# Attention groups merged across batches and put between W2-W1 pairs of waves, with z summed over j on VectorE and batch 0's first chunk ahead of all else

## The chip, the cores and the metric

The kernel runs on one core of a Trainium2 chip. The metric is the device time of one execution in microseconds (us). Most executions of a kernel agree closely, but some are longer (of eleven of the kernel before, run beside z_twice_b1, ten took 138.85 to 139.62 us and one 140.37). A run counts as *slow* when it is more than 1.5% above the fastest run of the same kernel, otherwise as *fast*. Ratios are made from fast runs alone; a median quoted for an experiment is that of all its runs. A kernel is called faster or slower when it differs by more than 2%.

A profile is one traced execution. The span inside it (first to last instruction) is about 2 us shorter than the timed value (136.9 of 139.2 us before).

## The reference

There are two parts, one after the other, all in float32 in and out.

```python
# attention without softmax: q, k, v are (B=4, H=4, S=1088, D=32); S1, S2 are (8, 32)
def phi(x):                                   # 8 x 8 = 64 features
    a = einsum('rd,bhsd->bhsr', S1, x)
    b = einsum('rd,bhsd->bhsr', S2, x)
    return einsum('bhsi,bhsj->bhsij', a, b).reshape(..., 64)
q_p, k_p = phi(q), phi(k)
kv  = einsum('bhsf,bhsd->bhfd', k_p, v)
z   = sum(k_p, axis=2)                        # over the sequence
num = einsum('bhsf,bhfd->bhsd', q_p, kv)
den = einsum('bhsf,bhf->bhs', q_p, z)[..., None] + 1e-06
x   = (num / den), heads side by side         # (4352 tokens, 128)

# feed-forward: w_in (128, 2048), w_out (2048, 128), beta (2048,)
h = x @ w_in
g = h / (1 + exp(-beta * h))
out = g @ w_out
```

## The kernel before

The kernel folds beta into the weights, so that ScalarE applies a plain silu. The second part is cut into 68 *waves*. A wave is one W1 step (two matmuls of 512 tokens by 128 hidden units into PSUM), one silu of 128x1024 on ScalarE (about 1.02 us each), and later one W2 step (two matmuls that add to the output). The kernel sets `manual_schedule` for TensorE, VectorE and ScalarE, so that their instruction order is the order of the program text. So the kernel interleaves by hand: the function `slot` issues a wave and one attention group.

An attention batch is made of these groups:

- `kps` projects k; VectorE turns the result (`kab`) and multiplies the two halves into the 64 features, `kp`. In `kp` the sequence lies as 9 pieces j on up to 128 partitions.
- `ab` makes the two projections of q: `aps`, which ScalarE copies to `asb`, and `bps`, which VectorE multiplies with it into `qp`. There are four pairs per batch: two chunks of the sequence by two pairs of heads.
- `kv` adds up kv and z in one PSUM tile `kvz`: for each j and head one matmul with v and one with a block of ones.
- `ndt` transposes kv and z, `den` makes the denominator (matmuls `dps`, then five VectorE steps in a row to its reciprocal `rb`), and `num` makes the numerator `nps` and the product `xT`. The waves of those tokens can start once `xT` is there.

```python
psm = tile_pool("psm", bufs=2, PSUM)     # "wave": W1 tiles and aps share two buffers
pso = tile_pool("pso", bufs=1, PSUM)     # "moeout": the output sums
ps2 = tile_pool("ps2", bufs=1, PSUM)     # "two": kps, bps, nps
ps1 = tile_pool("ps1", bufs=1, PSUM)     # "one": kvz, ndps, dps
...
def slot(group=None):                    # wave, then group, then W2 of earlier waves
    if moe["ci"] < len(tok_chk) and sum(tok_chk[moe["ci"]]) <= moe["ready"]:
        w1()
    if group is not None:
        group()
    todo = moe["todo"]
    if len(todo) == 2 and todo[0][1] == 0 and todo[0][0] > 0:
        return
    while len(todo) > 1:
        w2(*todo.pop(0))
...
# in kv: z by matmuls with ones
for j in j_list:
    kr = 64 if j == 0 else P
    for which in range(2):
        for h in range(H):
            nc.tensor.matmul(
                out=kvz[32 * h : 32 * h + 32, F * which : F * which + F],
                lhsT=v_t[b][:kr, h, j, :] if which == 0 else ones[:kr, :],
                rhs=kp[:kr, h, j, :], ...)
...
# the first chunk of batch 0
kps()
for h in range(H): outer(h, 0, 5)
ab((0, 0), None)()
for h in range(H): outer(h, 5, NJK)
ab((1, 0), (0, 0))()
prep_rbeta()
keep_warm(4)
kv([1, 2, 3, 4])()
ab(None, (1, 0))()
kv([5, 6, 7, 8, 0])()
...                                      # weights scaled on GpSimd
keep_warm(2); ndt(); turn_q(0, 1); keep_warm(2)
den(0)(); num(0)()
keep_warm(6)
...
for b in range(1, B):
    slot(kps)
    outer(0); outer(1)
    slot(ab((0, 0), None))
    outer(2)
    slot(ab((1, 0), (0, 0)))
    outer(3)
    turn_q(b, 1)
    slot(kv([1, 2]))
    slot(ab((0, 1), (1, 0)))
    slot(kv([3, 4]))
    slot(ab((1, 1), (0, 1)))
    slot(kv([5, 6]))
    slot(ab(None, (1, 1)))
    turn_k(b + 1)
    slot(kv([7, 8, 0]))
    slot(ndt)
    slot(den(0))
    slot(num(0))
    slot(den(1))
    slot(num(1))
    turn_q(b + 1, 0)
    slot()
while moe["ci"] < len(tok_chk):          # the drain: waves only
    slot()
```

`keep_warm(n)` issues n matmuls whose results nobody uses; they only keep TensorE busy.

## Time and profile before

| | before |
|---|---|
| timed, median (3 runs) | 139.22 us (139.01 to 139.24) |
| span in the profile | 136.9 us |
| first wave starts | 21.7 us |
| busy: TensorE / ScalarE / VectorE | 117.5 / 80.9 / 64.0 us |

The page's busy times of the kernel before (engine, busy us, share of the span, instructions; PEld is the load of the stationary operand, which overlaps PE: 117.5 and 46.5 us in a span of 136.9):

```profile
PE 117.5 (86%) x1407; PEld 46.5 (34%) x1407; DVE 64.0 (47%) x127; ACT 80.9 (59%) x96; POOL 11.6 (8%) x25
```

An average over the span hides the stages, so the span is cut where the `xT` of a batch's second chunk is done. Busy times by windows, before (from:to, its length, then the busy us of each engine with the number of instructions, the granted TensorE clock, the share of DMA engines busy, GB/s):

```profile
0.00:21.72 21.72, 17.72 (x242) 7.18 (x243) 12.12 (x33) 4.33 (x11) 8.03 (x19) 1.00 0.94 301
...
30.72:57.42 26.70, 22.86 (x327) 8.97 (x328) 15.48 (x30) 16.02 (x19) 0.00 (x0) 1.00 0.26 56
57.42:84.84 27.42, 25.57 (x340) 9.78 (x339) 15.47 (x30) 18.64 (x22) 0.00 (x0) 1.00 0.14 21
84.84:112.26 27.42, 25.57 (x340) 9.78 (x339) 14.25 (x28) 18.65 (x22) 0.00 (x0) 1.00 0.14 20
112.26:131.88 19.62, 17.00 (x85) 8.00 (x84) 1.44 (x3) 16.83 (x18) 0.00 (x0) 1.00 0.28 41
```

The lines are: the start, batches 1, 2 and 3, and the drain. In batch 2 TensorE (the first pair of numbers) is busy for 25.6 of 27.4 us and the others far less. In the drain each of 18 silu takes 1.09 us from start to start. ScalarE is busy for 1.02 us of that and waits 0.26 us for a wave after every second silu, so it all but sets the pace.

The chain of waits that ended last, before, in the start and around the denominators of batch 2 (start us, length us, what; "xN" instructions taken together):

```profile
11.86 0.67 DVE qp L368
12.53 0.17 DVE rbeta L184
...
12.75 1.64 PE kvz L386 x64
...
15.03 1.39 PE kvz L386 x80
...
21.72 0.61 PE wave L242 x2
...
77.31 0.69 PE dps L433 x8
...
79.05 0.79 DVE rb L449
...
79.94 0.77 DVE xT L475
...
80.75 0.59 PE wave L242 x2
```

The first `kvz` waits until 12.75 us for `rbeta`, the reciprocal of beta, which stands on VectorE behind a product `qp`. It needs the result of neither; `rbeta` holds it up because the transposed beta lies in the one PSUM buffer that `kvz` takes next. (Each float32 matmul of `kvz` stands in these views as two records: the program has 72 per batch, the trace 144.) From `dps` at 77.3 to the wave at 80.75 us the chain runs over VectorE, with TensorE having little to do. Only part of that shows up as a wait, since TensorE does have an `nps` and some wave work in between. The waits of TensorE, before (engine line <- what ended the wait: us in all, times, longest us):

```profile
PE wave L242 <- DVE xT L475: 3.9, 4, 2.1
PE moeout L206 <- ACT g L250: 2.7, 9, 0.7
PE wave L242 <- ACT g L250: 2.1, 4, 0.6
```

Of the 3.9 us, 0.5 are at the first wave, 2.1 in batch 1 and 0.6 in each of batches 2 and 3.

### The profile page before, as it was taken

Reading aid. Unit: us, or ns where it says so; the run is one execution under the profiler, and the core shown is the slowest. Engines: PE = TensorE matmul, PEld = TensorE weight load, DVE = VectorE, ACT = ScalarE, POOL = GpSimd, SP = SyncE. Lnnn points to the kernel's source line nnn. Section 1 sums busy time; section 2 is a strip of 40 time slices with the busy share of each in tenths; the row PEclk is TensorE's granted clock in tenths of the full one; section 3 lists DMA queues with packets and bytes.
Section 4 is the critical chain, followed back from the end, with each engine's and each line's share of the span. In section 5 each row is a group of like instructions: output and inputs, shape, how many; then the busy total and the mean of one; then the engine's idle time right before and its main releaser. Section 6 shows DMA issues by size and latency. Waiting matters only on the chain.

```text
span 136.9 us, 3341 instructions
## 1 busy us (share of the span) xinstructions
PE 117.5 (86%) x1407; PEld 46.5 (34%) x1407; DVE 64.0 (47%) x127; ACT 80.9 (59%) x96; POOL 11.6 (8%) x25
## 2 busy tenths in 40 slices
PE   5698986989889984998989989989899898889850
PEld 2124632323333431224334322233344233333530
DVE  0687273499642535976245459772423570100210
ACT  3411104766776632677675756776757478888940
POOL 4000599300000000000000000000000000000000
PEclk9999999999999999999999999999999999999999
DMA  4999999999441000140004001400130004022042
GB/s 141 293 293 416 379 325 262 260 222 254 77 66 25 0 5 0 17 62 5 0 10 71 1 0 20 62 0 5 19 58 5 0 13 63 0 43 41 10 66 38
DMA packets 22814, 12.41 MB, mean 91 GB/s; under 512 B 18688, under 2 KB 20752, under 8 KB 22544
## 3 DMA queue, kind: packets, MB, share of 16 engines
q1 hardware_dynamic: 22736, 12.19, 36.4%
q8 instruction: 11, 0.18, 0.6%
q14 instruction: 3, 0.02, 0.1%
q10 hardware_dynamic: 64, 0.01, 0.1%
HBM read 9.97 MB, written 2.23 MB: 89 GB/s over the span
## 4 chain that ended last, share of the span: by engine, by line
PE 59%; DVE 22%; ACT 10%; issue 3%; DMA 2%; ACTq 1%; DVEq 0%
PE moeout L206 18%; PE wave L242 17%; ACT g L250 10%; PE kvz L386 8%; PE aps L353 4%; DVE kp L327 3%; DVE rb L449 3%; PE dps L433 3%; PE bps L353 3%; PE kps L308 3%; DVE xT L475 3%; DVE qp L368 3%; DVE dT L442 2%; DMA sraw<-in_S_dram 2%; DVE o_sb L216 2%
## 5 line engine op out<-in xcount | busy, mean ns | idle before, releaser
L250 ACT ACTIVATE g<-wave 128x1024 f16<-128x1024 f32 x68 | 68.7, 1023 | 38.5 <-PE wave L242 38.1
L242 PE MATMUL wave<-xT,winp 128*128 128x512 f16 (+1 forms) x144 | 40.2, 367 | 6.0 <-DVE xT L475 3.9
L206 PE MATMUL moeout<-g,woutp 128*128 128x512 f16 (+1 forms) x144 | 39.8, 369 | 3.6 <-ACT g L250 2.7
L368 DVE TENSOR_TENSOR qp<-bps,asb 128x576 f32<-128x576 f32 (+1 forms) x16 | 11.6, 725 | 25.4 <-PE bps L353 24.4
L242 PEld LDWEIGHTS <-winp 128*128 128x128 f16 x144 | 13.7, 97 | 25.0 <-issue 12.4
L206 PEld LDWEIGHTS <-woutp 128*128 128x128 f16 x144 | 10.9, 97 | 23.7 <-issue 18.8
L216 DVE STREAM_TRANSPOSE o_sb<-moeout 128x512 f32<-128x512 f32 (+1 forms) x9 | 6.1, 673 | 22.1 <-PE moeout L206 22.1
L386 PE MATMUL kvz<-kp,v 128*32 128x64 f32 (+1 forms) x288 | 11.2, 232 | 1.4 <-DVE kp L327 1.1
L353 PE MATMUL aps<-qT,s_164 32*64 32x288 f32 (+1 forms) x128 | 12.2, 448 | 0.0
L363 ACT COPY asb<-aps 128x576 f32<-128x576 f32 (+1 forms) x16 | 9.7, 608 | 3.9 <-PE aps L353 3.4
L353 PE MATMUL bps<-qT,s_166 32*64 32x288 f32 (+1 forms) x128 | 11.8, 430 | 0.0
L327 DVE TENSOR_TENSOR kp<-kab 128x576 f32<-128x576 f32 (+2 forms) x20 | 11.4, 624 | 0.0
L386 PE MATMUL kvz<-kp,ones 128*32 128x64 f32 (+1 forms) x288 | 10.1, 226 | 0.0
L386 PEld LDWEIGHTS kvz<-kp,v 128*32 128x32 f32 (+1 forms) x288 | 6.9, 113 | 8.7 <-issue 4.2
L134 PE MATMUL warm<-idle 128*128 128x512 f16 x22 | 8.2, 517 | 1.5 <-POOL idle L129 1.5
L386 PEld LDWEIGHTS kvz<-kp,ones 128*32 128x32 f32 (+1 forms) x288 | 7.3, 115 | 0.0
L442 DVE STREAM_TRANSPOSE dT<-dps 128x288 f32<-128x288 f32 (+1 forms) x8 | 3.7, 461 | 6.8 <-PE dps L433 6.8
L173 POOL TENSOR_TENSOR winp<-w_in_sb,beta_bc 128x256 f16<-128x256 f32 x8 | 5.5, 732 | 13.1 <-DMA beta_bc<-in_moe_beta_dram 13.1
L449 DVE STREAM_TRANSPOSE rb<-rc 128x576 f32<-128x576 f32 (+1 forms) x8 | 6.0, 745 | 0.3
L353 PEld LDWEIGHTS aps<-qT,s_164 32*64 32x64 f32 x128 | 3.7, 138 | 6.9 <-issue 3.5
L475 DVE TENSOR_TENSOR xT<-nps,rb 128x576 f16<-128x576 f32 (+1 forms) x8 | 5.7, 710 | 0.5
L291 DVE STREAM_TRANSPOSE qT<-q 128x576 f32<-128x576 f32 (+1 forms) x8 | 5.8, 730 | 0.0
(43 smaller groups left out, 54.6 us busy)
## 6 DMA issues: line engine op xcount, KB each, us to landing
v<-in_v_dram SPq DMA_DIRECT2D x16, 144.0 KB, 7.7
k<-in_k_dram SPq DMA_DIRECT2D x3, 544.0 KB, 11.0
q<-in_q_dram SPq DMA_DIRECT2D x3, 544.0 KB, 11.4
out_dram<-o_sb SPq DMA_DIRECT2D x20, 64.0 KB, 2.0
w_in_sb<-in_moe_w_in_dram SPq DMA_DIRECT2D x1, 1024.0 KB, 7.5
beta_bc<-in_moe_beta_dram SPq DMA_DIRECT2D x1, 1024.0 KB, 9.5
k<-in_k_dram SPq DMA_DIRECT2D x1, 288.0 KB, 3.0
q<-in_q_dram SPq DMA_DIRECT2D x1, 288.0 KB, 4.6
```

The costliest lines, as they stand in the source:

```text
L134: nc.tensor.matmul(out=t, lhsT=idle[:, :P], rhs=idle, start=True, stop=True)
L206: nc.tensor.matmul(out=moe["acc"][:, :tw], lhsT=woutp[:, j, :], rhs=g[:, jj, :tw], start=(j == 0), stop=(j == NJ - 1),)
L216: nc.vector.transpose(out=o_sb[:, :nt, :].rearrange("p t d -> p (t d)"), in_=moe["acc"][:, :tw])
L242: nc.tensor.matmul(out=wv[:, jj * tw : (jj + 1) * tw], lhsT=winp[:, (j0 + jj) * P : (j0 + jj + 1) * P], rhs=xT[:, t0 : t0 + tw], start=Tru ...
L250: nc.scalar.activation(out=g, in_=wv, func=ACTF.Silu)
L327: nc.vector.tensor_tensor(out=kp[:, h, j0:j1].rearrange("p j (i l) -> p j i l", i=R), in0=bass.AP(tensor=a0.tensor, offset=a0.offset, ap=[ ...
L353: nc.tensor.matmul(out=dst[64 * c : 64 * c + 64, m, : 32 * tn], lhsT=sx[rows, :], rhs=qT[rows, t0 : t0 + tn, c, :], start=True, stop=True,)
L363: nc.scalar.copy(out=asb[:, :, :w], in_=aps[:, :, :w])
L368: nc.vector.tensor_tensor(out=qp[:, 2 * pb : 2 * pb + 2, 32 * t0 : 32 * t0 + w], in0=bps[:, :, :w], in1=st[b_of][:, :, :w], op=MUL,)
L386: nc.tensor.matmul(out=kvz[32 * h : 32 * h + 32, F * which : F * which + F], lhsT=v_t[b][:kr, h, j, :] if which == 0 else ones[:kr, :], rh ...
L449: nc.vector.transpose(out=rb[:, :tn].rearrange("p t c s -> p (t c s)"), in_=bass.AP(tensor=r0.tensor, offset=r0.offset, ap=[list(r0.ap[0]) ...
L475: nc.vector.tensor_tensor(out=xT[:, o : o + 2 * w].rearrange("p (t c s) -> p c t s", c=2, s=32), in0=nps[:, :, :w].rearrange("p c (t s) -> ...
```

## The change

Its intent is to (1) start the first wave sooner, (2) give TensorE enough other work while VectorE makes the reciprocals, and (3) take half of the `kvz` matmuls off TensorE.

- **z.** From batch 1 on VectorE adds the nine pieces of `kp` in four additions (`sum_z`), and one matmul per head with ones adds the partitions up.
- **Order.** Every slot is now group, then W2-W1 pairs, one or two of them. The next batch's `kps` and `kp` and its first `aps` run inside the present batch, so that no group has only `aps` or only `bps`.
- **Start.** `kv` follows the first half of `kp`; the products `qp` and the reciprocal of beta come later. S1 and S2 are loaded already spread over all partitions, the weights in two halves, and GpSimd's order is fixed by hand as well. The operand of the idle matmuls is filled on VectorE, with ones instead of zeros.

```diff
-    def slot(group=None):
-        if moe["ci"] < len(tok_chk) and sum(tok_chk[moe["ci"]]) <= moe["ready"]:
-            w1()
+    def slot(group, waves):
         if group is not None:
             group()
         todo = moe["todo"]
-        if len(todo) == 2 and todo[0][1] == 0 and todo[0][0] > 0:
-            return
-        while len(todo) > 1:
-            w2(*todo.pop(0))
+        for _ in range(waves):
+            if moe["ci"] < len(tok_chk) and sum(tok_chk[moe["ci"]]) > moe["ready"]:
+                break
+            lag = 3 if todo and todo[0][1] == 0 and todo[0][0] > 0 else 2
+            while len(todo) >= lag:
+                w2(*todo.pop(0))
+                lag = 2
+            if moe["ci"] < len(tok_chk):
+                w1()
+            ...
# z
-            for which in range(2):
+            for which in range(2 if zsum is None else 1):
 ...
+        if zsum is not None:
+            for h in range(H):
+                nc.tensor.matmul(out=kvz[32 * h : 32 * h + 32, F : 2 * F], lhsT=ones,
+                    rhs=zsum[:, h, :], start=False, stop=True, skip_group_check=True)
+    def sum_z(b):
+        kp = KP[b]
+        z4 = sbA.tile([P, H, 4, F], F32, tag="z4", name="z4", bufs=1)
+        nc.vector.tensor_tensor(out=z4, in0=kp[:, :, 1:5], in1=kp[:, :, 5:9], op=ADD)
+        nc.vector.tensor_tensor(out=z4[:, :, :2], in0=z4[:, :, :2], in1=z4[:, :, 2:], op=ADD)
+        zs = sbA.tile([P, H, F], F32, tag="zs", name="zs")
+        nc.vector.tensor_tensor(out=zs, in0=z4[:, :, 0], in1=z4[:, :, 1], op=ADD)
+        nc.vector.tensor_tensor(out=zs[:64], in0=zs[:64], in1=kp[:64, :, 0], op=ADD)
+        return zs
# the first chunk of batch 0 (the old order is above)
+    kps(0)
+    ab((0, 0, 0))
+    mult00 = ab((0, 1, 0), (0, 0, 0))
+    mult10 = ab(None, (0, 1, 0), (psm, "wave"))
+    prep_rbeta_mm = prep_rbeta()
+    for h in range(H): outer(0, h, 0, 5)
+    kv(0, [1, 2, 3, 4])
+    for h in range(H): outer(0, h, 5, NJK)
+    mult00(); mult10()
+    kv(0, [5, 6, 7, 8, 0])
+    prep_rbeta_mm()
 ...
+    keep_warm(2); ndt(0); keep_warm(3)
+    invert = den(0, 0); divide = num(0, 0); invert(); divide()
+    turn_q(0, 1)
+    keep_warm(9)
+    slot(None, 1)
+    slot(lambda: r_group((0, 0, 1), None), 1)
+    slot(lambda: r_group((0, 1, 1), (0, 0, 1)), 1)
+    turn_q(1, 0)
+    slot(lambda: r_group((1, 0, 0), (0, 1, 1)), 1)
+    slot(lambda: den(0, 1)(), 1)
+    slot(lambda: num(0, 1)(), 1)
+    turn_k(1)
+    slot(lambda: kps(1), 1)
# the batches (r_group is ab with its product at once)
+    for b in range(1, B):
+        more = b + 1 < B
+        few = b == 1
+        if b == 1:
+            for h in range(H): outer(b, h)
+        turn_q(b, 1)
+        slot(lambda: r_group((b, 1, 0), (b, 0, 0)), 1)
+        zs = sum_z(b)
+        slot(lambda: kv(b, [1, 2, 3, 4], zs), 1 if few else 2)
+        slot(lambda: r_group((b, 0, 1), (b, 1, 0)), 1)
+        turn_k(b + 1)
+        slot(lambda: kv(b, [5, 6, 7, 8, 0], zs), 1 if few else 2)
+        slot(lambda: r_group((b, 1, 1), (b, 0, 1)), 1)
+        turn_q(b + 1, 0)
+        if more:
+            slot(lambda: kps(b + 1), 1 if few else 2)
+            outer(b + 1, 0)
+        slot(lambda: r_group((b + 1, 0, 0) if more else None, (b, 1, 1)), 1)
+        if more: outer(b + 1, 1)
+        slot(lambda: ndt(b), 1 if few else 2)
+        if more: outer(b + 1, 2)
+        slot(lambda: den(b, 0)(), 1 if few else 2)
+        slot(num0_den1, 1)               # num(b, 0) and den(b, 1) together
+        if more: outer(b + 1, 3)
+        slot(lambda: num(b, 1)(), 1)
+    slot(None, 10**3)
```

## The prediction

> **What bounds it now.** The span is 136.9 us (timed median 139.22: 2.3 outside). The chain of waits shows four stages.
> 1. Start, 0 to 21.7 us: a latency chain. The kvz matmuls wait until 12.75 for the reciprocal of beta, queued on VectorE behind a product; the first wave starts at 21.72.
> 2. Batch 0, second chunk, to 30.8.
> 3. Three batch periods: 27.6, 27.4, 26.0 us. In the second (58.35 to 85.78, by windows) TensorE is busy 25.6 us, ScalarE 18.7, VectorE 15.5, for 16 waves: TensorE-bound, with holes. The largest is the denominator chain: after dps, VectorE needs 2.7 us while TensorE has one group to do; the next wave waits 0.6 to 2.1 us on xT.
> 4. Drain, 111.8 to 131.9: 18 waves, ScalarE-bound at 1.095 us each (TensorE needs about 0.9); then 5 us of tail.
>
> Busy time overstates TensorE[...]: a pair recorded as 0.59 us takes 0.43 in the chain.
>
> **What the change does.**
> - From batch 1 on it removes 36 of 72 kvz matmuls per batch and adds 4: about 1.15 us of TensorE per batch (32 cost 0.58 in the chain). It adds four VectorE additions: at 0.69 us per 576 elements start to start, 1,024, 512, 256 and 256 elements come to about 2.45 us (estimate). VectorE grows from 15.5 to about 18 us per batch, in total from 64 to about 71.
> - Merged batches: groups with only aps or only bps go, and the next batch's kps and kp run inside this one. Two waves cover kvz, ndt, den, so the 2.7 us chain is hidden.
> - Start: kvz begins after the first half of kp; products and rbeta come later. First wave at about 19.0 (estimate).
>
> **Sum by stage**, slot costs read off the chain (aps+bps group with one W2-W1 pair 1.75 us, kvz 1.6, den 1.55, num 1.65, each further wave 0.9), which reproduce before's 27.4.
> - Start 19.0; batch 0 with kps of batch 1: 10.7 (before 9.1 without kps).
> - Batch 1: 11 waves, but VectorE has two sets of kp plus z, about 21.2 us in one in-order queue: VectorE-bound, 22.
> - Batch 2: 16 waves, 23.3, TensorE-bound (ScalarE 20.4, VectorE 18).
> - Batch 3: 14 waves, no next batch: 20.8.
> - Drain: 20 waves, with the silu in flight 23 us, ScalarE-bound; tail 5.
>
> Span about 124, plus 2.3: **126 us**, 80% range **121 to 131.5**. Faster by over 2% 0.93, within 2% 0.05, slower 0.02. Nearly all is on the critical path: periods 2 and 3 about 9 us, batch 1 about 5, start about 2.5; the longer drain gives 2 back.
>
> **What will show it right or wrong.** First wave between 18 and 20 us; kvz records with ones down from 288 to 72, plus 24 for zs; last 20 silu 1.09 us apart; waits of waves on xT nearly gone after batch 1; in batch 1 TensorE waiting on kp, qp or zs with VectorE over 90% busy.
>
> **What would make it wrong.** Faster: batch 1 may take 19. Slower: the single PSUM buffer of bps, kps and nps may hold TensorE up in batches 2 and 3 (behind z a product is 2.4 us late); ScalarE may limit where two waves follow a group, since aps and waves share two PSUM buffers; the start may be held by v's arrival, or by TensorE's half-rate first microseconds (matmuls 0.43 us apart until about 13.8).

## The result and the profile after

| | before | after |
|---|---|---|
| timed, median (4 runs each, side by side) | 139.23 us (139.01 to 140.3) | 131.38 us (130.22 to 132.02) |
| span in the profile | 136.9 us | 130.2 us |
| first wave starts | 21.7 us | 22.3 us |
| from the first wave to the end | 115.2 us | 107.9 us |
| busy: TensorE / ScalarE / VectorE | 117.5 / 80.9 / 64.0 us | 113.1 / 79.8 / 71.3 us |

The ratio is 0.9412, with a 95% interval from 0.9322 to 0.9503: faster. A ratio is the mean time of one kernel's fast runs over that of the other's fast runs of the same rounds, so it is not quite the ratio of the medians quoted. The profiled execution of the change took 132.02 us, the longest of its four. That matters below, because its start is a late one.

The page's busy times after:

```profile
PE 113.1 (87%) x1216; PEld 45.9 (35%) x1216; DVE 71.3 (55%) x142; ACT 79.8 (61%) x92; POOL 11.1 (9%) x24
```

VectorE grew by 7.3 us, as predicted (71). Busy times by windows, after, cut at the same events (the same columns):

```profile
0.00:22.34 22.34, 18.35 (x243) 8.63 (x244) 11.92 (x36) 3.51 (x7) 8.09 (x20) 1.00 0.96 274
...
31.81:55.67 23.86, 21.79 (x276) 8.20 (x276) 21.61 (x40) 15.21 (x18) 0.00 (x0) 1.00 0.44 93
55.67:80.82 25.15, 23.64 (x274) 8.97 (x274) 17.79 (x34) 18.54 (x22) 0.00 (x0) 1.00 0.15 23
80.82:102.08 21.26, 20.56 (x243) 8.16 (x243) 12.44 (x25) 15.44 (x19) 0.00 (x0) 1.00 0.18 26
102.08:125.00 22.92, 19.82 (x96) 9.04 (x94) 2.15 (x3) 20.35 (x21) 0.00 (x0) 1.00 0.24 35
```

The three batches went from 26.7, 27.4 and 27.4 us to 23.9, 25.2 and 21.3 us. The drain got 3.3 us longer, because more waves are left for it, at the same pace. In batch 1 VectorE (the third pair) is now busy for 91% of the time and TensorE for as much.

The chain of waits, after, in the start and around the denominators of batch 2:

```profile
12.06 0.76 DVE qp L388
...
12.90 4.13 PE kvz L406 x144
...
22.34 0.60 PE wave L259 x2
...
74.02 0.62 PE dps L471 x8
74.64 0.54 PE moeout L223 x2
75.18 0.43 PE wave L259 x2
75.61 0.43 PE moeout L223 x2
76.04 0.43 PE wave L259 x2
76.47 0.65 PE nps L506 x16
```

Around the denominators the chain no longer leaves TensorE: two W2-W1 pairs stand between `dps` and `nps`. In the start, `kvz` began no earlier than before (12.90 against 12.75 us) and took 4.13 us where before it took 1.64 + 1.39 us. The waits of TensorE, after:

```profile
PE moeout L223 <- ACT g L267: 3.1, 11, 0.7
PE kps L327 <- DVE kT L303: 2.3, 2, 1.4
PE aps L369 <- ACT g L267: 2.0, 5, 0.7
```

The wait of waves on `xT`, 3.9 us before, is in no line any more. A new one is there: `aps` waits for a silu, since `aps` and waves share two PSUM buffers.

So after the first wave the change took 7.3 us away (115.2 to 107.9), and before it, in this execution, it added 0.6 us. These are the two questions of the experiments: what the 7.3 us are made of, and why the start did not come at 19 us.

### The profile page after: what moved, and what is told of

Same layout as the page of the kernel before. It is cut to its first block, busy times and chain, and to the rows that moved or that the text cites. A ratio compares the mean times of both kernels' runs of the same rounds, so it can differ in the third digit from the quotient of the medians.

```text
span 130.2 us, 2977 instructions
## 1 busy us (share of the span) xinstructions
PE 113.1 (87%) x1216; PEld 45.9 (35%) x1216; DVE 71.3 (55%) x142; ACT 79.8 (61%) x92; POOL 11.1 (9%) x24
## 4 chain that ended last, share of the span: by engine, by line
PE 49%; DVE 22%; ACT 15%; DMA 5%; issue 5%; SPq 1%; ACTq 0%; DVEq 0%
PE moeout L223 15%; ACT g L267 15%; PE wave L259 13%; PE kvz L406 5%; DMA q<-in_q_dram 5%; PE aps L369 4%; DVE kp L346 4%; PE dps L471 3%; DVE qp L388 3%; PE bps L369 2%; DVE rb L489 2%; DVE xT L516 2%; PE nps L506 2%; PE kps L327 2%; DVE qT L315 2%
## 5 line engine op out<-in xcount | busy, mean ns | idle before, releaser
L267 ACT ACTIVATE g<-wave 128x1024 f16<-128x1024 f32 x68 | 67.8, 1023 | 30.1 <-PE wave L259 29.7
L223 PEld LDWEIGHTS <-woutp 128*128 128x128 f16 x144 | 11.4, 97 | 24.8 <-issue 18.8
L233 DVE STREAM_TRANSPOSE o_sb<-moeout 128x512 f32<-128x512 f32 (+1 forms) x9 | 6.1, 676 | 21.5 <-PE moeout L223 21.5
L369 PE MATMUL aps<-qT,s_165 32*64 32x288 f32 (+1 forms) x128 | 13.6, 448 | 3.1 <-ACT g L267 2.0
L406 PE MATMUL kvz<-kp,v 128*32 128x64 f32 (+1 forms) x288 | 9.1, 246 | 1.2 <-DVE qp L388 0.8
L147 PE MATMUL warm<-idle 128*128 128x512 f16 x23 | 7.6, 479 | 1.5 <-DVE hm L159 1.5
L369 PEld LDWEIGHTS aps<-qT,s_165 32*64 32x64 f32 x128 | 4.6, 138 | 10.5 <-ACT g L267 5.3
L327 PE MATMUL kps<-kT,sk 64*32 64x288 f32 x64 | 3.9, 482 | 2.3 <-DVE kT L303 2.3
L506 PE MATMUL nps<-qp,nd 64*32 64x288 f32 (+1 forms) x128 | 5.5, 401 | 0.0
```

What stands on the lines that cost most here:

```text
L223: nc.tensor.matmul(out=moe["acc"][:, :tw], lhsT=woutp[:, j, :], rhs=g[:, jj, :tw], start=(j == 0), stop=(j == NJ - 1),)
L267: nc.scalar.activation(out=g, in_=wv, func=ACTF.Silu)
L369: nc.tensor.matmul(out=dst[64 * c : 64 * c + 64, m, : 32 * tn], lhsT=sx[rows, :], rhs=qT_of[bb][rows, t0 : t0 + tn, c, :], start=True, sto ...
L406: nc.tensor.matmul(out=kvz[32 * h : 32 * h + 32, F * which : F * which + F], lhsT=v_t[b][:kr, h, j, :] if which == 0 else ones[:kr, :], rh ...
L506: nc.tensor.matmul(out=nps[32 * h : 32 * h + 32, c, :w], lhsT=ND[b][rows, 32 * h : 32 * h + 32], rhs=QP[b][rows, h, 32 * t0 : 32 * t0 + w] ...
```

## The experiments

Theory A is the prediction's: VectorE binds batch 1, TensorE batches 2 and 3, and the order hides the denominators. Its rival B is that z on VectorE costs as much as it saves, or that VectorE binds more of the kernel than batch 1. For the start, theory A is that DMA holds v back, and its rival is that TensorE runs at half rate and the chain is bound by instruction order.

All twelve runs gave correct results. The stages are cut as in the windows above; "first wave" is read in each kernel's profiled execution.

| kernel | fast runs / all | ratio to before (95%) | first wave, us | batch 1 / 2 / 3, us |
|---|---|---|---|---|
| the change | 4 / 4 | 0.9412 (0.9322 to 0.9503) | 22.3 | 23.9 / 25.2 / 21.3 |
| z_twice_b1 | 4 / 6 | 0.9796 (0.9754 to 0.9838) | 20.8 | 29.2 / 25.1 / 21.3 |
| z_twice_b2 | 4 / 6 | 0.9436 (0.9394 to 0.9478) | 20.5 | 23.9 / 25.5 / 21.3 |
| z_b1_off | 3 / 6 | 0.9483 (0.943 to 0.9536) | 20.0 | 25.1 / 25.1 / 21.2 |
| w_gate | 1 / 6 | none | 21.1 (slow) | 25.2 / 25.1 / 21.3 (slow) |
| after_again | 5 / 6 | 0.937 (0.9324 to 0.9416) | 19.8 | 23.9 / 25.2 / 21.2 |
| warm | 4 / 6 | 0.9426 (0.9382 to 0.9469) | 21.5 | 23.9 / 25.1 / 21.3 |
| z_off | 3 / 6 | 0.9556 (0.9498 to 0.9614) | 19.8 | 24.5 / 25.9 / 22.0 |
| before_z | 6 / 6 | 0.9821 (0.9783 to 0.9858) | 20.7 | 27.4 / 26.8 / 26.7 |
| old_start | 4 / 6 | 0.9475 (0.9413 to 0.9537) | 23.7 (slow) | 23.9 / 25.1 / 21.3 (slow) |
| idle4 | 2 / 6 | 0.9407 (0.9335 to 0.9478) | 19.4 | 23.9 / 25.1 / 21.2 |
| even | 1 / 6 | none | 22.1 (slow) | 23.9 / 24.8 / 20.7 (slow) |
| even_idle4 | 2 / 6 | 0.9274 (0.9202 to 0.9347) | 20.3 | 23.9 / 24.8 / 20.7 |

The batches repeat to 0.02 us between the change and its second run, although the chips and the starts differ. So where stages are compared, a difference of a few tenths counts. This holds for slow profiles too: in those of old_start and even, the time from the first wave to the end was 107.9 and 107.0 us, against 107.9 us in the change. What made these two runs slow lies in the start alone, so their batches may be read, but their first waves may not be compared with fast ones.

### z_twice_b1: the additions of z twice, in batch 1

```diff
         zs = sum_z(b)
+        if b == 1:
+            zs = sum_z(b)
```

> The four VectorE additions of z are done twice in batch 1 only (the first result is thrown away). If batch 1 is bound by VectorE's queue, as the prediction has it, the stage from kps of batch 1 to the last xT of batch 1 grows from 21.8 us by the 2.7 us that the additions took in the trace (38.67 to 41.51 less gaps), and the time by about 2.5 us, 2%. If TensorE or ScalarE bounds it, it grows by less than 0.5 us.

Measured: 136.73 us (median of 6 runs), ratio 0.9796; batch 1 grew by 5.3 us, from 23.9 to 29.2. The sign is as expected, the size is about twice that. Two lines of its views tell why. The first is from the waits of TensorE in batch 1; the second is a window of the busy times, with the granted clock third from the end:

```profile
PE kvz L418 <- DVE zs L445: 2.6, 1, 2.6
```

```profile
43.00:50.00 7.00, 7.00 (x53) 1.75 (x45) 4.39 (x8) 3.00 (x4) 0.00 (x0) 0.57 0.26 40
```

TensorE waited 2.6 us for the sum, and in the 7 us after that wait its granted clock was 0.57 in the mean (1.00 in the 9.4 us after them); the first two `wave` matmuls took 0.97 us there on the chain of waits, against 0.43 us further on. The batch grew by twice the wait. Added VectorE work in batch 1 is on the critical path. The size does not measure VectorE alone. That the wait brings such a slow spell on is not shown, and other waits differ: after one of 2.1 us in batch 1 before_z has a spell (two `wave` matmuls are recorded with 1.01 us) and the kernel before has none (0.59 us), and after one of 2.4 us idle4 has none (0.59 us).

### z_twice_b2: the same in batch 2

```diff
         zs = sum_z(b)
+        if b == 2:
+            zs = sum_z(b)
```

> The same doubling in batch 2 only. If batch 2 is bound by TensorE and ScalarE (VectorE busy 16.2 of 23.6 us), the time changes by less than 0.6 us. If the single queue of VectorE matters everywhere, it grows by about 2.5 us as in batch 1.

Measured: 131.57 us, ratio 0.9436, not to be told from the change's 0.9412. Batch 2 grew by 0.4 us for about 2.8 us of added VectorE work (from the start of the first addition to that of the next step). So VectorE does not bind batch 2, and rival B's second half falls.

### z_b1_off: z of batch 1 back on TensorE

```diff
-        zs = sum_z(b)
+        zs = sum_z(b) if b > 1 else None
```

> z of batch 1 is summed by the ones matmuls on TensorE again, batches 2 and 3 keep the additions. If batch 1 is VectorE-bound, the 2.7 us of additions leave the binding queue and the 1.0 us of matmuls go to an engine with slack: 1.5 to 2.5 us faster, about 1.5%. If TensorE binds it, 1 us slower.

Measured: 133.26 us, ratio 0.9483, and batch 1 took 25.1 us instead of 23.9. This is a miss: it should have become shorter if VectorE alone bound batch 1. About half of the 1.2 us belongs to this execution: the second group of `kvz` took 2.03 us here and 1.39 us in z_off below, which has the same program in batch 1, and 0.35 us of that is a stall that the profile puts down to nothing ("issue"). In z_off batch 1 grew by 0.6 us; that is what the additional `kvz` matmuls on TensorE cost. Adding to VectorE in batch 1 costs, and taking from it brings nothing, which fits two engines that are nearly balanced. By the ratios alone (0.9483 against 0.9412, with intervals that overlap) the loss is not shown.

### w_gate: the loads of the weights held behind v of batch 0

```diff
+    nc.vector.memset(w_in_sb[:, :1], 0.0)     # after turn_q(0, 0); the loads must wait for it
     for c in range(0, DFF, DFF // 2):         # all loads of weights and of batches 1 to 3,
         ...                                   # moved here from before the constants
```

> The weight loads wait for a one-column memset on VectorE placed behind the first qT, so that they are issued at about 8.5 us rather than 5.55 and don't share the DMA engines with v of batch 0. If v's arrival (12.7 us by its issue and its time to landing) is what holds the first kvz at 12.9 us, v lands at about 10, kvz starts at about 11.0 (first half of kp) and the first wave comes 1.3 to 2 us earlier, unless the weights then come too late. If kvz waits for the product on VectorE that the profile names, kvz still starts at 12.9 and nothing is gained.

Measured: five of six runs were slow, the one fast run took 132.09 us, and there is no ratio. The profile fell in the slow state too. In it `kvz` still waited 1.1 us for v, until 11.88 us, although the weight loads could not start before the memset at 8.2 us; that is within the range in which `kvz` began in the other traces (10.4 to 12.9 us, see after_again), so this one trace gives no sign that the weights are what delays v. And q of batch 1 came so late that `aps` waited 3.2 us for it: here the loads that were put off had to be paid for later. One slow profile decides neither question.

### after_again: the change unaltered, on another chip

There is no edit.

> The changed kernel unchanged, for its spread and for a second trace of its start. In the five traces so far the first wave came at 22.3, 20.8, 20.5, 20.0 and 21.1 us with the same code up to there (but for the weights in the last). If that is chance of the run, the same kernel shows another start here, and times between 130 and 135 us. If it belongs to the edits, the first wave comes at 22.3 again and the times stay within 130.2 to 132.0.

Measured: 130.81 us (before, on that chip: 139.02), ratio 0.937. The first wave came at 19.84 us, 2.5 us sooner than in the first profile, with the same instructions; from there to the end it took 107.9 us, exactly as long. So the start differs from one execution to the next, and the rest doesn't. Two neighbouring groups of `kvz` matmuls on the timeline, first in the change's profile and then in that of after_again (start us, length us, engine, line, operation, tiles, shapes, number; in brackets the idle time before and its releaser):

```profile
13.08 0.47 PE L406 MATMUL kvz<-kp,ones 128*32 128x64 f32 x8
13.29 0.47 PE L406 MATMUL kvz<-kp,v 128*32 128x64 f32 x8
```

```profile
10.36 0.32 PE L406 MATMUL kvz<-kp,v 128*32 128x64 f32 x8 [0.42 <-DVE kp L346]
10.47 0.32 PE L406 MATMUL kvz<-kp,ones 128*32 128x64 f32 x8
```

In the first the groups of eight start 0.21 us apart, in the second 0.11 us: half rate and full rate. The same two rates are seen elsewhere: in the change's profile the idle matmuls at the very start come 0.43 us apart and the nine before the first wave 0.22 us, and `kvz` fell on either side of this step. The granted clock does not always show it: over `kvz` it reads 1.00 in the change's profile (12.9 to 16.9 us), and 0.51 in z_twice_b2 (11.2 to 14.7 us), whose groups start 0.21 us apart as well. So the rate is read here from the distance between matmuls. Over the seven traces with an unaltered start (the change, z_twice_b1, z_twice_b2, z_b1_off, after_again, z_off, even), `kvz` began between 10.4 and 12.9 us and ran at half rate in four; the first wave came between 19.8 and 22.3 us, at 20.8 in the mean (20.5 without even, a slow run). Two traces with the old start gave 21.7 and 20.7.

What held the first `kvz` was v: its last load (issue plus time to landing) landed at 10.1 us in after_again, 11.9 in even and 12.7 in the change's profile, each time 0.2 to 0.3 us before `kvz` began (10.36, 12.14 and 12.90 us). In z_off, z_b1_off, z_twice_b2 and z_twice_b1 `kvz` began at 10.56, 10.62, 11.21 and 11.59 us. The half rate goes with the lateness: the three that began by 10.6 us ran at full rate, the four from 11.2 us on at half rate. In the change's profile all nine idle matmuls at the start are 0.43 us apart and take 4.02 us together; in the other three of the four they take only 3.48 to 3.66 us, so that the last of them came faster, and `kvz` ran at half rate there all the same. That lateness is the cause is not shown: idle4, with the same program up to there, began at 11.26 us and ran at full rate (groups 0.11 us apart), although its nine idle matmuls took 4.02 us.

The profile does not always name v. In that of the change the wait is put down to `qp`, but in the program the first `kvz` waits for v and the first half of `kp` alone. In the trace of even the wait is put down to v outright:

```profile
PE kvz L406 <- DMA v<-in_v_dram: 1.9, 1, 1.9
```

There is another loss in after_again. Here are steps of its chain of waits shortly before the first wave:

```profile
15.34 0.60 PE nps L506 x3
15.94 1.31 issue
17.25 0.71 PE nps L506 x13
17.96 2.05 PE warm L147 x9
```

TensorE stops after 3 of 16 `nps` matmuls for 1.31 us and waits for nothing that the profile shows, and then nine idle matmuls stand before the wave.

### warm: more idle matmuls before `kvz`, to see whether it then runs at full rate

```diff
-    keep_warm(9)
+    keep_warm(11)
...
     mult10 = ab(None, (0, 1, 0), (psm, "wave"))
+    keep_warm(4)
     prep_rbeta_mm = prep_rbeta()
```

> Eleven idle matmuls at the start instead of nine, and four more ahead of the beta transposition, where TensorE waits for kp and v anyway. If TensorE's half rate in the kvz of batch 0 (4.0 us in the trace of the change, 2.3 in the runs where it was warm) is the part of the start that I mis-sized, kvz takes 2.3 us here in every trace and the first wave comes at 20.5 or earlier, 1 to 1.5 us off the median. If v's arrival is the whole of it, the time stays.

Measured: 131.66 us, ratio 0.9426; no gain. In the profile `kvz` took 2.35 us, at full rate. But v came as early there as in after_again (its loads took 4.6 to 5.1 us to land, and 5.0 to 5.4 us in after_again), where `kvz` ran at full rate without the edit; and the four idle matmuls, which ended at 11.2 us, themselves kept `kvz` until 11.55. So the trace does not show whether the edit helps where v is late. The stall came back in another place of the chain:

```profile
11.55 2.35 PE kvz L406 x144
...
15.73 0.68 PE dps L471 x5
16.41 1.62 issue
18.03 0.69 PE dps L471 x3
```

It stands after 5 of 8 `dps`: six matmuls earlier in the program than in after_again, and the edit put exactly six matmuls ahead of it. So in these two traces the stall goes with the number of matmuls issued, not with an operation. The traces of z_off, z_b1_off, w_gate and idle4 have it too, at 1.0 to 1.2 us and after 3 of 16 `nps`. What it is was not shown. The DMA engines were full at the time (from 14 to 18 us their packets came to 100 to 120% of the 16 engines' time in each microsecond in after_again, and to 99 to 113% in warm). One packet of the kind that the profile calls instruction, about 16 KB, moved between 14 and 15 us in after_again, before the stall from 15.9 us, and between 15 and 16 us in warm, before the stall from 16.4 us. The change's profile has such a packet between 16 and 17 us and no stall, but it comes to `dps` only at 18.87 us. A link between the packet and the stall was not tried and is not shown.

### z_off: z on TensorE in all batches, the rest of the change kept

```diff
-        zs = sum_z(b)
+        zs = None
```

> The new order, but z by the ones matmuls in all batches. By the prediction's sum z on VectorE is worth about 1 us in each of batches 2 and 3 and costs in batch 1; after z_b1_off (stage 23.7 rather than 22.5 us) I expect about 1.2 us more in each of the three batches by the traces, so 2.5 to 3.5 us slower than the change. If the order alone made the gain, the time stays within 0.7 us.

Measured: 134.45 us, ratio 0.9556. Its fast runs have a mean of 133.06 us, against 130.50 us of after_again on the same chip: 2.6 us. The three batches grew by 0.60, 0.74 and 0.76 us. That is the `kvz` matmuls on the chain of waits; here is batch 2 in z_off and then in the change:

```profile
56.11 1.03 PE kvz L406 x64
...
61.49 1.39 PE kvz L406 x80
```

```profile
57.00 0.58 PE kvz L406 x32
...
61.96 0.83 PE kvz L406 x40
62.79 0.25 PE kvz L418 x8
```

With 36 `kvz` matmuls of v and four of `zs` a batch's `kvz` costs about 1.66 us of TensorE, against 2.42 us with all 72, so 0.76 us less. Some 2.1 to 2.6 us of the whole gain are therefore z, and the first half of rival B falls as well. In batch 1 z brings 0.6 us although VectorE is full there.

### before_z: z on VectorE in the kernel before, the order left alone

```diff
-                    for which in range(2):
+                    for which in range(2 if b == 0 else 1):
...
+                if 0 in j_list and b > 0:         # the four matmuls of zs with ones
...
         turn_q(b, 1)
+        sum_z()
         slot(kv([1, 2]))
```

> The old order and the old start, with z summed on VectorE from batch 1 on. Old batches have VectorE busy 15.5 of 27.4 us and TensorE on the chain, so the 1.0 us of matmuls per batch should come off the path: 139.1 to about 136.5 us, a ratio near 0.98. If the additions delay the products that TensorE waits for, there is no gain or a loss.

Measured: 136.71 us, so 2.3 us less than before. The ratio 0.9821 (0.9783 to 0.9858) is clear of 1, though a gain of 2% is not. Batches 2 and 3 are 0.65 and 0.75 us shorter, as in z_off. Batch 1 is 0.65 us longer: a spell at half rate from 52.1 to about 55 us lies in it (two `wave` matmuls are recorded with 1.01 us, against 0.59 us before and after). In this one profile 1.0 us of the gain is an earlier first wave (20.7 against 21.7 us), whose program is the same, so the 2.3 us may hold some luck of the start. By the stages z is worth as much in the old order as in the new, and the order is the rest.

### old_start: the new order of the batches after the old order of batch 0's first chunk

```diff
     kps(0)
-    ab((0, 0, 0))
-    mult00 = ab((0, 1, 0), (0, 0, 0))
-    mult10 = ab(None, (0, 1, 0), (psm, "wave"))
-    prep_rbeta_mm = prep_rbeta()
     for h in range(H):
         outer(0, h, 0, 5)
-    kv(0, [1, 2, 3, 4])
+    ab((0, 0, 0))
     for h in range(H):
         outer(0, h, 5, NJK)
+    mult00 = ab((0, 1, 0), (0, 0, 0))
     mult00()
+    prep_rbeta()()
+    keep_warm(4)
+    kv(0, [1, 2, 3, 4])
+    mult10 = ab(None, (0, 1, 0))
     mult10()
     kv(0, [5, 6, 7, 8, 0])
...                                            # and the old order of ndt, den, num with 2 + 2 + 6 idle matmuls
```

> The new order of groups from the first wave on, but batch 0's first chunk in the order of before: product before kvz, the beta reciprocal ahead of kvz in the same PSUM buffer, kvz split by a bps group. The loads and the S preparation stay new. If the reordered start is worth what the fast traces of the change show (first wave at 19.8 against 21.7 before), this is 1 to 2 us slower than the change, 132 to 133 us. If the loads, and not the order, set the first wave, the two agree within 0.7 us.

Measured: 132.49 us, ratio 0.9475 (0.9413 to 0.9537). The change's own ratios are 0.9412 and 0.937, with intervals that overlap this one. Against the mean of those two the old order is about 1.2 us longer (0.0084 of 139 us), and by the widths of the intervals the new order of the start is worth anything from nothing to a little over 2 us. The 2.7 us that the prediction gave it are not there. The profile is of a slow run and is not used. The new way of loading S1, S2 and the weights was kept, so this experiment says nothing on that.

### idle4: four idle matmuls before the first wave instead of nine

```diff
-    keep_warm(9)
+    keep_warm(4)
```

> Four idle matmuls instead of nine behind the first nps. In the fast traces nps ends at 17.9, the first chunk of xT at 18.8, and the first wave starts only at 19.84, when nine idle matmuls are through. I expect the first wave at 18.8 to 19.0 where the start is fast, nothing where it is slow, and 0.5 to 1 us off the median. If TensorE falls to half rate for want of those matmuls, the first waves get longer and it is slower.

Measured: 132.55 us, of which two of six runs fast, ratio 0.9407; no gain. The first wave came at 19.4 us, the earliest of all traces, and did not run slower for want of the five idle matmuls (0.59 us for its two matmuls, as in the change). The time was given back a little later, as the chain of waits shows:

```profile
13.67 11.21 DMA q<-in_q_dram
...
24.90 0.79 DVE qT L315
...
25.82 0.42 PE aps L369
```

The q of batch 1 landed at 24.9 us, and the `aps` that works one batch ahead waited 2.4 us for it. In the change's profile, with its late start, the `aps` waits for `qT` came to 1.1 us in all. A part of what the start gains is turned into a wait for DMA.

### even: the second wave put behind a q group instead of `kv` and `kps`, in batches 2 and 3

```diff
-        slot(lambda: r_group((b, 1, 0), (b, 0, 0)), 1)
+        slot(lambda: r_group((b, 1, 0), (b, 0, 0)), 1 if few else 2)
         zs = sum_z(b)
-        slot(lambda: kv(b, [1, 2, 3, 4], zs), 1 if few else 2)
-        slot(lambda: r_group((b, 0, 1), (b, 1, 0)), 1)
+        slot(lambda: kv(b, [1, 2, 3, 4], zs), 1)
+        slot(lambda: r_group((b, 0, 1), (b, 1, 0)), 1 if few else 2)
         turn_k(b + 1)
-        slot(lambda: kv(b, [5, 6, 7, 8, 0], zs), 1 if few else 2)
-        slot(lambda: r_group((b, 1, 1), (b, 0, 1)), 1)
+        slot(lambda: kv(b, [5, 6, 7, 8, 0], zs), 1)
+        slot(lambda: r_group((b, 1, 1), (b, 0, 1)), 2 if more and not few else 1)
         turn_q(b + 1, 0)
         if more:
-            slot(lambda: kps(b + 1), 1 if few else 2)
+            slot(lambda: kps(b + 1), 1)
```

> In batches 2 and 3 the second wave stands behind the aps and bps group instead of behind kvz and kps, the number of waves unchanged. The trace has TensorE waiting 1.4 us in batch 2 and 0.6 us in batch 3 for a silu that still holds the PSUM buffer of aps (and the chain through ScalarE there). If those waits are real costs, batches 2 and 3 get 1 to 2 us shorter together and the time falls by about 1 us; if TensorE's own work binds, less than 0.4 us.

The purpose was to take away the wait of `aps` on the silu, 2.0 us in the change. Measured: five of six runs were slow and there is no ratio; the fast run took 128.84 us. The profile is of a slow run, but its batches are those of the fast profile of even_idle4 (24.8 and 20.7 us). In it the wait is gone from the list, and batches 2 and 3 are 0.36 and 0.52 us shorter. The two microseconds of waiting were thus worth 0.9 us: most of it only stood where TensorE would have waited at the next place.

### even_idle4: both together

The edit is that of even and that of idle4.

> Both of the last two edits. If they add up, 1.5 to 2.5 us less than the change: 128.5 to 129.5 us. If the drain or the start absorbs one of them, no better than the better one.

Measured: two fast runs, 129.38 and 128.66 us, ratio 0.9274 (0.9202 to 0.9347). This is the lowest ratio of all, but its interval overlaps that of after_again (0.9324 to 0.9416), with few fast runs. It is likely a little better than the change; that it is, was not shown.

## Why the prediction was right or wrong

The predicted time was 126 us with a range up to 131.5, and 131.38 us was measured. Faster was right and the mechanism in the batches was right, but the point was 5.4 us low: a gain of 13 us was predicted and 7.8 us came. That the median lies inside the range, by 0.1 us, is in part luck, since the four runs go from 130.22 to 132.02 us. Here is the sum term by term, against the profiled execution of the change (132.02 us). The stages are cut here as the prediction cut them, where the first group of the next stage begins on TensorE:

| term | predicted | measured |
|---|---|---|
| start, to the first wave | 19.0 | 22.3 |
| batch 0 with `kps` of batch 1 | 10.7 | 12.4 |
| batch 1 | 22 | 20.2 |
| batch 2 | 23.3 | 25.2 |
| batch 3 | 20.8 | 21.5 |
| drain | 23 | 23.3 |
| tail | 5 | 5.2 |
| outside the span | 2.3 | 1.8 |

**The failed step is the start: "kvz begins after the first half of kp; products and rbeta come later. First wave at about 19.0 (estimate)."** It is the largest error, 3.3 us in this execution. In place of it, the runs showed a start that varies from 19.8 to 22.3 us for the same instructions, at 20.8 in the mean. So a gain of 2.7 us was predicted, and the traces give about 0.5 us in the mean against the two old starts (20.8 against 21.2 us); old_start put it at about 1.2 us in the timed runs, with a wide interval. Four things were seen in traces to take part in it: v lands between 10.1 and 12.7 us, so that `kvz` can't always follow the half of `kp`; `kvz` may run at half rate (4.1 us, against 2.5 us in after_again), and did in the four of these seven where `kvz` began latest (from 11.2 us on); where both go well, TensorE stalls 1.0 to 1.6 us, in five traces at the same `nps` and in warm six matmuls earlier in the program, and idle matmuls follow; and what is won can come back as a wait on q of batch 1 (idle4, 2.4 us). The prediction had named the first two among its risks but had not put them in the sum. What stays open: how much each of the four is worth, why v lands early or late (the loads of S1 and S2, now 16 KB each, and the order of the queue were not tried by themselves), and what the stall is.

**Batch 0, 1.7 us too small.** The `kps` of batch 1 waited 1.4 us for the transposed k, which stands behind `xT` in VectorE's order. Before, the transposition of k stood ahead of the denominators' steps on VectorE, and `kps` waited only 0.4 us, for `xT`. So the new order made this wait, and the sum did not count it.

**Batch 1, "VectorE-bound, 22": half right.** Doubling z there lengthened the batch, but taking z away did not shorten it (z_b1_off, and z_off with +0.6 us). VectorE and TensorE end nearly together. The term was 1.8 us too large, which hid part of the other errors in the sum, and a part of VectorE's work went over the boundary: the first `bps` of batch 2 began only after the last `xT` of batch 1, at 55.7 instead of 55.0 us.

**Batches 2 and 3, 1.9 and 0.7 us too small.** In batch 2, 0.7 us is that spill and 1.4 us is `aps` waiting for a silu, the risk that the prediction named ("aps and waves share two PSUM buffers"). But even showed that taking the waits away returns only 0.36 us in batch 2 and 0.52 in batch 3. The rest of the error in batch 2 is not separated further.

**What held.** The denominators' chain is hidden: the waits of waves on `xT` fell from 3.9 us (3.4 of it after the first wave) to none. The records of `kvz` with ones fell from 288 to 72, plus 24 for `zs`. z saves less than predicted, 0.76 us of TensorE per batch (1.15), and its additions take 2.8 us of VectorE from start to start (2.45). VectorE does not bind batch 2 (z_twice_b2). In the drain the silu are 1.095 us apart and the last 20 waves took 23.3 us (23).

Where the gain came from, then: the time after the first wave fell by 7.3 us. z is 2.1 us of that by the stages (z_off) and 2.3 to 2.6 by the timed runs of z_off and before_z. The order of the groups is the remaining 5 us or so. It is a difference of what the batches gained (against before, z_off's are 2.2, 1.5 and 5.4 us shorter, the last also because it leaves waves to the drain) and what the drain and batch 0 gave back (3.3 and 0.5 us). Which part of the order brought how much (the hidden denominators, the merged groups, the `kps` of the next batch) was not tried apart; the waits on `xT` after the first wave were 3.4 us. Together with about 0.5 us of the start this makes the 7.8 us measured, although the start's share rests on few traces.

## What to carry to other kernels

When a group ends in a long chain on another engine, put enough independent work of the bound engine between its two ends, and check in the waits that the wait is gone and has not become another one. Before moving work from one engine to another, ask of each stage how far the second engine is from binding it: the same four additions cost 0.4 us when doubled in batch 2 and 5.3 us in batch 1. A gain at the start of a kernel, where here the share of DMA engines busy was 0.96 over the first 22.3 us and `kvz` took 4.1 us in one trace and 2.5 us in another, should enter a prediction with the range that several traces of the same code show, and not as the difference of two chains.
